# Raw words of the MLP weights in a room of their own, loaded one chunk ahead, converted among the first sequence's steps

## The chip, the core and the metric

The kernel runs on one core of a Trainium2 chip, with its five engines: TensorE (PE, matmuls; its weight loads are shown as PEld), VectorE (DVE), ScalarE (ACT), GpSimd (POOL) and SyncE (SP), whose queue issues all DMAs of this kernel. The metric is the device time of one execution in microseconds; what is compared is the median over runs.

## What is computed

The reference takes eight sequences of 3136 positions and 256 features. It is a spectral layer followed by a mixing layer with an MLP, cut here to what matters:

```python
X = np.fft.rfft(x, axis=1)                      # attention part
Yr = Xr @ w_r - Xi @ w_i + b_r
Yi = Xr @ w_i + Xi @ w_r + b_i
Yr, Yi = soft_threshold(Yr, 0.01), soft_threshold(Yi, 0.01)
x = np.fft.irfft(Yr + 1j * Yi, n=3136, axis=1)
mixed = np.real(np.fft.fft(np.fft.fft(x, axis=1), axis=2))
u = x + mixed
un = (u - mean(u)) / np.sqrt(var(u) + 1e-06)
out = u + np.maximum(un @ w_ch1, 0.0) @ w_ch2    # 256 -> 1024 -> 256
```

The MLP weights `w_ch1` and `w_ch2` come as 64-bit floats and reach the kernel as pairs of 32-bit words. Before the first MLP matmul the kernel has to make of them two single-precision parts, a high and a low one, with integer and float instructions.

## The kernel before

The sequence transform is split as 3136 = 64 x 49. Each sequence b goes through three parts, written as Python generators:

- `p1`: the transform over 64, from `in_x` (tile `xf`) by matmul (`g_f`) into `ev` and out to DRAM (`ad`). For b = 0 it is `p1_first`.
- `p2`, in four frequency steps q. `p2_f2` loads `af` (from `ad`) and the table `tff`, and does the transform over 49 (line 427); `p2_w` multiplies by the spectral weights (`g_w`, lines 150 to 152 by way of `mm3`), adds the bias (line 489, tile `y`) and thresholds; `p2_mix` forms sums `ef`, multiplies (`g_mix`, line 546) and combines the rows in `mq` on VectorE, GpSimd and ScalarE (lines 559 to 568), and stores them to DRAM (`md`, lines 573 to 587); `p2_yt` and `p2_g2` go back over 49 (table `tif`, result `bd`).
- `p3`, in groups of 3 or 4 rows: `p3_norm` loads `bf` (from `bd`) and `mt` (from `md`), does the last inverse transform (`g_g`, from the parts `bh` and `bl`), adds `mt` (line 691, tile `ut`) and normalizes (line 709, tile `nm`); `p3_tr` transposes (`g_ut`, line 727); `p3_mlp1` and `p3_mlp2` are the MLP (`h`, lines 150 to 152 and 746, 747; `o`).

Nearly every matmul from the second step on is done three times on split operands (`mm3`: high with low, low with high, high with high). The first sequence's own transforms over 64 and 49 and back are done once, on unsplit operands.

The order comes from two places. Each generator yields a due time in units where one sequence takes T = 10000, and a heap takes the piece of work with the earliest due time next. The first sequence's frequency steps have due times 1.0, 1.13, 1.26 and 1.39 T and run on for about 0.4 T each; its `p3` begins at 2.0 T, the second sequence's `p2` at 1.77 T. The framework's scheduler then sets the order on each engine. Every engine works through its own instructions in that order, and so does SP with its DMAs. A tile stands in a room that its tag names, with a number of buffers; an instruction that writes a buffer waits until the last reader of its earlier content is done. `behind(1, ...)` puts a DMA on SP's queue after the `af` load number 1.

`weights` loads and converts the MLP weights in eight chunks of 128 x 512 values (128 x 1024 words), four of `w_ch1` and four of `w_ch2`, due at 1.5 T and on in steps of 0.0525 T. `split_double` does one chunk. Its raw words stand in the tag `uth`, which the second and fourth frequency steps of the first sequence (`x_tiles`) and later the transposed MLP input use as well; its temporaries stand in `mt` and `ut`, which `p3_norm` uses as well. One chunk is one load, one Abs on ScalarE (line 169), seven instructions on VectorE (lines 170, 172, 174, 175, 178, 180, 182), one cast on ScalarE (line 186, the high part) and two instructions on GpSimd (lines 188 and 189, the low part).

## Time and profile before

| | |
|---|---|
| median of 3 runs | 1952.38 us (1949.41 to 1956.86) |
| the profiled execution's own time | 1949.14 us |
| its span | 1947.4 us |
| mean granted TensorE clock | 0.976 |
| PE busy | 1836.5 us (94%) |
| DVE busy | 1323.5 us (68%) |
| ACT busy | 850.1 us (44%) |
| POOL busy | 707.7 us (36%) |
| time of DMA packets, share of 16 engines' span | 42.3% (230.82 MB) |

A row of a group gives line, engine, operation, tiles (output and inputs), shapes and count, then busy us and mean ns of one, then the idle time of the engine before them and what ended it. Rows of the timeline give start and duration in us; "x4" merges four neighbours. A row of waits gives who waited for whom, the sum in us, the number of times and the longest. In the page's slices of 48.7 us each, TensorE is nearly full from the sixth on and has its holes in the first five.

### The profile page before, as it was taken

To read this page: it belongs to the slowest core of one execution; us is meant where nothing else is said; L and a number is where in the kernel's file an instruction comes from. 1 tells how busy PE (TensorE), PEld (TensorE's weight loads), DVE (VectorE), ACT (ScalarE), POOL (GpSimd) and SP (SyncE) were. 2 spreads that over 40 slices of the span, in tenths; PEclk is the share of its full clock that TensorE was granted. 3 is DMA by queue.
4 is the path that set the end of the run, shared out by engine and by line. 5 is a ranking of instruction groups with operands and counts; after the bars stand their busy time and mean duration, and the time that the engine had idled before them with its cause. 6 is when DMAs were issued, how large, how long until landed. Compare 5 with 4: busy or idle time off the path is not lost.

```text
span 1947.4 us, 34761 instructions
## 1 busy us (share of the span) xinstructions
PE 1836.5 (94%) x12115; PEld 1693.2 (87%) x12115; DVE 1323.5 (68%) x2831; ACT 850.1 (44%) x1888; POOL 707.7 (36%) x1087
## 2 busy tenths in 40 slices
PE   4972799999999999999999999999999999999999
PEld 2862799989999999998999999998999999998999
DVE  2677688767767677767677676666777776675543
ACT  2553454445444454444444444444544434433322
POOL 0336453344433344343333443324533332322210
PEclk7995899999999999999999999999999999999999
DMA  8685444255443544435443453435443333223210
GB/s 221 168 236 160 106 135 133 81 142 139 115 123 109 146 137 113 115 99 148 128 136 103 122 150 104 132 101 149 127 116 104 97 109 90 79 73 113 63 41 25
DMA packets 163538, 233.03 MB, mean 120 GB/s; under 512 B 27484, under 2 KB 107428, under 8 KB 163364
## 3 DMA queue, kind: packets, MB, share of 16 engines
q1 hardware_dynamic: 163364, 230.82, 42.3%
q8 instruction: 96, 1.57, 0.3%
q14 instruction: 78, 0.64, 0.1%
HBM read 127.95 MB, written 102.76 MB: 118 GB/s over the span
## 4 chain that ended last, share of the span: by engine, by line
PE 80%; DVE 6%; DMA 6%; SPq 3%; issue 2%; POOL 1%; ACT 1%; DVEq 0%; POOLq 0%; ACTq 0%
PE o L151 8%; PE o L150 8%; PE o L152 8%; PE h L150 8%; PE h L151 8%; PE h L152 8%; PE g_f L427 4%; PE g_w L150 3%; PE g_w L152 3%; PE g_w L151 3%; PE g_yt L617 2%; PE g_g L150 2%; PE g_g L152 2%; PE g_g L151 2%; PE g_ut L727 2%
## 5 line engine op out<-in xcount | busy, mean ns | idle before, releaser
L151 PE MATMUL o<-w2h,hl 128*128 128x256 f32 x1568 | 430.3, 284 | 9.7 <-DVE hl L747 9.7
L747 DVE SCALAR_TENSOR_TENSOR hl<-h,hh 128x512 fp32r<-128x512 f32 (+1 forms) x416 | 272.3, 655 | 236.9 <-ACT hh L746 235.7
L746 ACT ACTIVATE hh<-h 128x512 fp32r<-128x512 f32 (+1 forms) x416 | 237.7, 572 | 438.4 <-PE h L152 381.6
L152 PE MATMUL o<-w2h,hh 128*128 128x256 f32 x1568 | 422.5, 279 | 0.0
L150 PE MATMUL o<-w2l,hh 128*128 128x256 f32 x1568 | 396.7, 285 | 4.5 <-DVE ut L766 2.8
L150 PE MATMUL h<-utl,w1h 128*128 128x512 f32 (+1 forms) x832 | 322.8, 388 | 6.6 <-DVE hl L747 6.6
L152 PE MATMUL h<-uth,w1h 128*128 128x512 f32 (+1 forms) x832 | 316.7, 381 | 0.0
L151 PE MATMUL h<-uth,w1l 128*128 128x512 f32 (+1 forms) x832 | 316.4, 380 | 0.0
L151 PEld LDWEIGHTS o<-w2h,hl 128*128 128x128 f32 x1568 | 295.9, 189 | 16.5 <-DVE hl L747 11.8
L150 PEld LDWEIGHTS o<-w2l,hh 128*128 128x128 f32 x1568 | 284.9, 189 | 17.9 <-ACT Xsh L436 2.9
L152 PEld LDWEIGHTS o<-w2h,hh 128*128 128x128 f32 x1568 | 295.8, 189 | 3.2
L147 POOL TENSOR_TENSOR bl<-bf,bh 128x512 fp32r<-128x512 f32 x104 | 129.7, 1247 | 301.9 <-ACT bh L686 301.7
L152 PEld LDWEIGHTS h<-uth,w1h 128*128 128x128 f32 x832 | 156.5, 188 | 23.9
L150 PEld LDWEIGHTS h<-utl,w1h 128*128 128x128 f32 x832 | 156.7, 188 | 21.4 <-DVE hl L747 7.5
L147 POOL TENSOR_TENSOR xl<-xf,xh 128x512 fp32r<-128x512 f32 (+1 forms) x75 | 98.5, 1313 | 202.1 <-ACT xh L370 197.1
L427 PEld LDWEIGHTS g_f<-tff,af 98*128 98x128 f32 x1024 | 144.5, 199 | 30.7 <-issue 20.4
L427 PE MATMUL g_f<-tff,af 98*128 98x100 f32 x1024 | 151.2, 278 | 20.9 <-DMA tff<-c_tf 11.9
L151 PEld LDWEIGHTS h<-uth,w1l 128*128 128x128 f32 x832 | 156.8, 188 | 13.5
L147 POOL TENSOR_TENSOR Xl<-xx,Xh 128x400 fp32r<-128x400 f32 (+1 forms) x96 | 107.6, 1123 | 83.6 <-ACT Xh L436 65.6
L691 DVE TENSOR_TENSOR ut<-g_g,mt 128x512 f32<-128x512 f32 x104 | 68.3, 657 | 96.1 <-PE g_g L152 69.9
L147 POOL TENSOR_TENSOR Xsl<-xs,Xsh 128x200 fp32r<-128x200 f32 x120 | 76.9, 641 | 153.3 <-ACT Xsh L436 144.2
L709 DVE TENSOR_SCALAR nm<-ut,ag,rs 128x256 f32<-128x256 f32 x196 | 90.0, 498 | 52.3 <-POOL rs L706 51.9
(155 smaller groups left out, 3793.2 us busy)
## 6 DMA issues: line engine op xcount, KB each, us to landing
bd<-bev SPq DMA_DIRECT2D x128, 196.0 KB
af<-ad SPq DMA_DIRECT2D x62, 392.0 KB
bf<-bd SPq DMA_DIRECT2D x184, 128.0 KB
out_dram<-ut SPq DMA_DIRECT2D x92, 256.0 KB
xf<-in_x SPq DMA_DIRECT2D x176, 128.0 KB
ad<-ev SPq DMA_DIRECT2D x168, 128.0 KB
md<-mq SPq DMA_DIRECT2D x112, 192.0 KB
mt<-md SPq DMA_DIRECT2D x416, 32.0 KB
```

The lines of the kernel that those rows point to most:

```text
L147: gp.tensor_sub(out_, full, hi.bitcast(F32))
L150: te.matmul(o, lh, rl, start=start, stop=False)
L151: te.matmul(o, ll, rh, start=False, stop=False)
L152: return te.matmul(o, lh, rh, start=False, stop=stop)
L427: te.matmul(g[:, o:o + 100], afs[s][:, ui * D + k * 128:ui * D + k * 128 + 128], tfs[s][:, ui], start=True, stop=True)
L617: te.transpose(gt[:100, (v * 2 + o) * 128:(v * 2 + o + 1) * 128], y[:, o, place].rearrange("p c j -> p (c j)"), ident)
L691: va.tensor_add(ut[:, :n], g[:, :w].rearrange("p (n d) -> p n d", d=D), mt[:, :n])
L709: va.tensor_scalar(nm[:, j], ut[:, j], ag[:, j, 0:1], rs[:, j], op0=ALU.subtract, op1=ALU.mult)
L727: te.transpose(gv[:, k, j * 128:(j + 1) * 128], nm[:, j, k * 128:(k + 1) * 128], ident)
L746: sc.activation(hh[:, :w], h[:, :w], AF.Relu)
L747: va.scalar_tensor_tensor(hl[:, :w], h[:, :w], 0.0, hh[:, :w].bitcast(F32), op0=ALU.max, op1=ALU.subtract)
```

## The change

The raw words of a chunk now take two tiles of 128 x 512 words, one in the tag `hh` and one in the tag `bf`, with two buffers each. Both tags exist before; until the first MLP matmul and the first `p3_norm` they stand mostly empty. The instructions that read raw words (the Abs on ScalarE, lines 174 and 180 on VectorE) are therefore done in two halves of 256 values. The load of chunk j + 1 is issued ahead of the conversion of chunk j. The due times become 1.14 T and on in steps of 0.065 T, so that all eight fall into the first sequence's frequency steps. The tiles of the converted weights are allocated at that earlier place. All values computed are the same.

```diff
@@ -122,6 +122,9 @@
 SHAPE0, STEP0 = (1.0, 1.069, 0.988), 0.13
 SHAPE, STEP1, STEP = (0.395, 0.569, 0.36), 0.2, 0.25
 START1, LEAD = 1.77, 1.48
+
+W_AT, W_STEP = 1.14, 0.065
+W_PAD = 32
 MLAG, NRM, TR = 0.874, -1.239, -0.993
 
 
@@ -162,22 +165,23 @@
         def tmp(tag, bufs, dt=I32):
             return sb.tile([128, 512], dt, tag=tag, bufs=bufs, name=f"cv_{name}_{tag}")
 
-        raw = sb.tile([128, 1024], I32, tag="uth", bufs=2, name="raw_" + name)
-        behind(1, out=raw.rearrange("p (f e) -> p f e", f=src.shape[1]), in_=src)
-        lo, hi = raw[:, 0::2], raw[:, 1::2]
+        halves = [(t[:, 0::2], t[:, 1::2], np.s_[:, 256 * e:256 * e + 256]) for e, t in enumerate(src)]
         tf = tmp("mt", 2, F32)
-        sc.activation(tf, hi.bitcast(F32), AF.Abs)
+        for lo, hi, at in halves:
+            sc.activation(tf[at], hi.bitcast(F32), AF.Abs)
         va.tensor_scalar(tf, tf, HI_MIN, HI_MAX, op0=ALU.max, op1=ALU.min)
         t = tf.bitcast(I32)
         va.tensor_scalar(t, t, 3, 0x7FFFFFFF, op0=ALU.logical_shift_left, op1=ALU.bitwise_and)
         w = tmp("ut", UTB)
-        va.tensor_scalar(w, hi, -0x80000000, 0x40000000, op0=ALU.bitwise_and, op1=ALU.bitwise_or)
+        for lo, hi, at in halves:
+            va.tensor_scalar(w[at], hi, -0x80000000, 0x40000000, op0=ALU.bitwise_and, op1=ALU.bitwise_or)
         va.tensor_tensor(w, w, t, op=ALU.bitwise_xor)
         wf = w.bitcast(F32)
         e = tmp("ut", UTB)
         va.tensor_scalar(e, w, -0x800000, None, op0=ALU.bitwise_and)
         r = tmp("mt", 2)
-        va.tensor_scalar(r, lo, 8, None, op0=ALU.logical_shift_right)
+        for lo, hi, at in halves:
+            va.tensor_scalar(r[at], lo, 8, None, op0=ALU.logical_shift_right)
         rf = tmp("ut", UTB, F32)
         va.scalar_tensor_tensor(rf, r, 2.0 ** -44, e.bitcast(F32), op0=ALU.mult, op1=ALU.mult)
 
@@ -770,18 +774,33 @@
     def weights():
         w1v = w1.bitcast(I32).rearrange("(k p) f -> p k f", p=128)
         w2v = w2.bitcast(I32).rearrange("(f p) e -> p f e", p=128)
-        parts1 = [(np.s_[:, k, q * 512:q * 512 + 512], w1v[:, k:k + 1, q * 1024:q * 1024 + 1024])
-                  for k in range(2) for q in range(2)]
-        parts2 = [(np.s_[:, f:f + 2, :], w2v[:, f:f + 2]) for f in range(0, 8, 2)]
-        for i, (name, shape, loads) in enumerate((("w1", [128, 2, FF], parts1), ("w2", [128, 8, D], parts2))):
-            if i:
-                sb.tile([128, 32], F32, tag="pad", bufs=1, name="pad")
-            h = sb.tile(shape, F32R, tag=f"W{2 * i}", bufs=1, name=name + "h")
-            l = sb.tile(shape, F32R, tag=f"W{2 * i + 1}", bufs=1, name=name + "l")
-            mlp_w[name] = h, l
-            for j, (sl, src) in enumerate(loads):
-                yield T * (1.5 + 0.42 * (4 * i + j) / 8)
-                split_double(name, h, l, sl, src)
+
+        todo = [("w1", np.s_[:, k, q * 512:q * 512 + 512], [w1v[:, k, (2 * q + e) * 512:(2 * q + e + 1) * 512] for e in range(2)])
+                for k in range(2) for q in range(2)]
+        todo += [("w2", np.s_[:, f:f + 2, :], [w2v[:, f + e] for e in range(2)]) for f in range(0, 8, 2)]
+        raw = {}
+
+        def load(j):
+            name, sl, srcs = todo[j]
+            raw[j] = []
+            for e, tag in enumerate(("hh", "bf")):
+                t = sb.tile([128, 512], I32, tag=tag, bufs=2, name="raw_" + name)
+                behind(1, out=t, in_=srcs[e])
+                raw[j].append(t)
+        yield T * (W_AT - W_STEP)
+        load(0)
+        for j, (name, sl, _) in enumerate(todo):
+            yield T * (W_AT + W_STEP * j)
+            if j % 4 == 0:
+                i, shape = ((0, [128, 2, FF]), (1, [128, 8, D]))[j // 4]
+                if i and W_PAD:
+                    sb.tile([128, W_PAD], F32, tag="pad", bufs=1, name="pad")
+                h = sb.tile(shape, F32R, tag=f"W{2 * i}", bufs=1, name=name + "h")
+                l = sb.tile(shape, F32R, tag=f"W{2 * i + 1}", bufs=1, name=name + "l")
+                mlp_w[name] = h, l
+            if j + 1 < len(todo):
+                load(j + 1)
+            split_double(name, h, l, sl, raw.pop(j))
 
 
     tasks = [load_small(), load_consts(), weights()]
```

The framework's scheduler makes these orders of it. First SP's queue behind the stores of the first sequence's `p1` (`ad`); `raw_w` is a raw load, and in the change a number in a name tells the two tiles of a chunk apart. Before:

```order
L336 DMA ad_82<-ev 2x24x256
L413 DMA tff<-c_tf 98x400 x2
L262 DMA tif<-c_ti 100x392 x2
L413 DMA tff<-c_tf 98x400
L411 DMA af<-ad_81 98x1024 x2
L262 DMA xf<-in_x 64x512 x4
L411 DMA af<-ad_81 98x1024
```

Now:

```order
L340 DMA ad_80<-ev 2x24x256
L266 DMA raw_w_263<-in_w 128x512
L266 DMA raw_w_265<-in_w 128x512
L417 DMA tff<-c_tf 98x400 x2
L266 DMA raw_w_321<-in_w 128x512
L266 DMA raw_w_323<-in_w 128x512
L417 DMA tff<-c_tf 98x400
L415 DMA af<-ad_79 98x1024 x2
L266 DMA xf<-in_x 64x512 x4
L266 DMA raw_w_424<-in_w 128x512
L266 DMA raw_w_426<-in_w 128x512
L415 DMA af<-ad_79 98x1024
```

The first two chunks' loads stand ahead of the `af` loads of the second frequency step, the third's ahead of the next one, and the two `tif` loads have moved behind them.

Second, VectorE around the first bias add (`y`) of the first sequence. Before:

```order
L454 TENSOR_TENSOR xs<-g_f_275,im 128x200
L144 TENSOR_TENSOR Xl<-g_f_275,Xh 128x2x200
L489 SCALAR_TENSOR_TENSOR y_341<-g_w,bias,ks 128x400
L491 TENSOR_SCALAR m<-y_341 128x400
L492 TENSOR_TENSOR Y<-y_341,m 128x8x50
L449 TENSOR_TENSOR xs<-xx 128x200 x2
L489 SCALAR_TENSOR_TENSOR y_379<-g_w,bias,ks 128x400
```

Now, `cv_w` being the conversion's temporaries and 424 and 426 the third chunk's tiles:

```order
L184 TENSOR_SCALAR cv_w_mt<-raw_w_424 128x256
L177 TENSOR_SCALAR cv_w_ut<-raw_w_426 128x256
L184 TENSOR_SCALAR cv_w_mt<-raw_w_426 128x256
L172 TENSOR_SCALAR cv_w_mt<-cv_w_mt 128x512
L174 TENSOR_SCALAR cv_w_mt<-cv_w_mt 128x512
L493 SCALAR_TENSOR_TENSOR y_369<-g_w,bias,ks 128x400
L178 TENSOR_TENSOR cv_w_ut<-cv_w_ut,cv_w_mt 128x512
L495 TENSOR_SCALAR m<-y_369 128x400
```

Two whole chunks and six instructions of the third (24 in all) stand ahead of the first bias add; from there to just behind the ninth bias add, VectorE's instructions of the other chunks alternate with those of the frequency steps.

Third, VectorE at the first sequence's last combination of rows (`mq_1277` before, `mq_1415` now). Before:

```order
L559 TENSOR_TENSOR mq_1277<-g_mix_1464,mq_1277 100x1
L562 TENSOR_TENSOR mq_1277<-mq_1277 100x4x64 x2
L178 TENSOR_SCALAR cv_w1_ut_1197<-cv_w1_ut_1194 128x512
L449 TENSOR_TENSOR xs_1526<-xx_1527 128x200
L182 SCALAR_TENSOR_TENSOR cv_w1_ut_1201<-cv_w1_mt_1199,cv_w1_ut_1197 128x512
L174 TENSOR_SCALAR cv_w1_ut_1284<-raw_w1_1278 128x512
L180 TENSOR_SCALAR cv_w1_mt_1289<-raw_w1_1278 128x512
L170 TENSOR_SCALAR cv_w1_mt_1280<-cv_w1_mt_1280 128x512
L144 TENSOR_TENSOR til_1822<-tif_1819,tih_1821 100x392
L172 TENSOR_SCALAR cv_w1_mt_1280<-cv_w1_mt_1280 128x512
L567 COPY mq_1277<-mq_1277 100x4x127
```

Now:

```order
L563 TENSOR_TENSOR mq_1415<-g_mix_1542,mq_1415 100x1
L566 TENSOR_TENSOR mq_1415<-mq_1415 100x4x64 x2
L453 TENSOR_TENSOR xs_1604<-xx_1605 128x200
L571 COPY mq_1415<-mq_1415 100x4x127
L453 TENSOR_TENSOR xs_1632<-xx_1633 128x200
L695 TENSOR_TENSOR ut_1582<-g_g1_1578,mt_1565 128x512
```

The conversion's instructions are gone from between the combination and the first `ut` of `p3_norm`. TensorE's own instructions keep nearly the same order up to there and have the same one later.

## The prediction

> **What bounds the kernel now.** I read the page's slices first, then windows cut where the program's steps change, then the waits. The windows of core 0 (columns: stretch and length, busy us and instructions of each engine, granted TensorE clock, DMA share, GB/s):
>
> ```profile
> 36.00:51.50 15.50, 6.52 (x28) 6.27 (x28) 2.98 (x6) 4.21 (x12) 4.45 (x6) 0.53 0.80 207
> 51.50:88.70 37.20, 34.99 (x208) 29.98 (x208) 24.95 (x56) 22.19 (x63) 13.24 (x23) 1.00 0.63 174
> 88.70:120.00 31.30, 30.28 (x177) 25.79 (x177) 19.76 (x45) 18.11 (x49) 10.91 (x15) 1.00 0.69 195
> 120.00:142.60 22.60, 14.09 (x73) 10.53 (x72) 19.66 (x33) 12.43 (x29) 12.09 (x9) 0.92 0.89 263
> 142.60:153.10 10.50, 1.87 (x10) 1.62 (x8) 8.11 (x18) 4.98 (x13) 8.05 (x6) 0.50 0.85 257
> 153.10:214.10 61.00, 22.81 (x87) 20.39 (x87) 38.52 (x64) 17.12 (x32) 32.41 (x35) 0.58 0.43 117
> 214.10:1947.40 1733.30, 1707.16 (x11495) 1587.99 (x11493) 1201.41 (x2597) 762.63 (x1677) 626.33 (x992) 1.00 0.40 112
> ```
>
> TensorE bounds two stretches: from 51.5 to 120 us, where it is idle 3.2 of 68.5 us, and from 214.1 to the end, idle 26 of 1733. Between 120 and 214.1 it works 38.8 of 94.1 us, much of it at a granted clock near 0.5. Nothing this change touches can win more than those 55 idle us and the slow clock. The waits of TensorE between 120 and 215 us name what it stands for:
>
> ```profile
> PE g_ut L727 <- DVE nm L709: 24.5, 2, 13.0
> PE g_g L150 <- POOL bl L147: 22.3, 1, 22.3
> ```
>
> Both are the entry into the MLP of the first sequence: its inverse transform waits for `bl`, its transposes for the normalized rows. What makes these late is the conversion, whose eight chunks fill VectorE and GpSimd just there. VectorE's groups of that stretch (columns: busy us, mean ns):
>
> ```profile
> L174 DVE TENSOR_SCALAR cv_w_ut<-raw_w 128x512 int32<-128x512 int32 x8 | 8.4, 1048 | 0.7 <-DMA raw_w<-in_w 0.7
> L182 DVE SCALAR_TENSOR_TENSOR cv_w_ut<-cv_w_mt,cv_w_ut 128x512 f32<-128x512 int32 x8 | 7.5, 937 | 0.3
> L178 DVE TENSOR_SCALAR cv_w_ut<-cv_w_ut 128x512 int32<-128x512 int32 x8 | 6.9, 860 | 0.3
> L180 DVE TENSOR_SCALAR cv_w_mt<-raw_w 128x512 int32<-128x512 int32 x8 | 6.7, 836 | 0.0
> L170 DVE TENSOR_SCALAR cv_w_mt<-cv_w_mt 128x512 f32<-128x512 f32 x8 | 6.5, 811 | 0.8 <-ACT cv_w_mt L169 0.7
> L175 DVE TENSOR_TENSOR cv_w_ut<-cv_w_ut,cv_w_mt 128x512 int32<-128x512 int32 x8 | 5.8, 725 | 0.2
> L172 DVE TENSOR_SCALAR cv_w_mt<-cv_w_mt 128x512 int32<-128x512 int32 x8 | 4.3, 539 | 0.1
> ```
>
> The means add up to 5.76 us a chunk, 46 us in all. The last chunk ran with GpSimd quiet; its VectorE time in the windows of `cv_w_ut` and of `cv_w_mt` (VectorE first):
>
> ```profile
> 194.00:199.00 5.00, 2.24 (x4) 0.62 (x1) 0.79 (x1) 0.82 0.07 19
> 194.00:199.00 5.00, 2.65 (x5) 0.68 (x1) 0.82 0.07 19
> ```
>
> Lines 175 and 182 write one and read the other, so they stand in both, at 0.69 us each in that chunk: 2.24 + 2.65 - 1.38 = 3.5 us is the quiet price, against 5.76 on average.
>
> **The change part by part.** The order of TensorE's instructions is nearly row for row the same up to the MLP and identical later, so I move the times of a fixed chain and ask how much earlier the first MLP matmul (214.14) comes. All times are of the profiled execution, 1949.1 us with a span of 1947.4; the median of the runs shown, 1952.4, lies 3.2 above it.
>
> *Loads ahead of the second frequency step.* Four raw loads now stand before the `af` loads that TensorE waits for, and two `tif` loads move behind.
>
> ```profile
> raw_w<-in_w SPq DMA_DIRECT2D x8, 512.0 KB
> tif<-c_ti SPq DMA_DIRECT2D x11, 153.1 KB
> 38.00:47.00 9.00, 0.03 (x1) 0.02 (x1) 1.70 (x4) 1.74 (x7) 3.08 (x5) 0.50 0.84 216
> PE g_f L427 <- DMA af<-ad: 9.0, 1, 9.0
> ```
>
> Two chunks of 512 KB less two of 153 KB are 718 KB or 0.74 MB; at the 216 GB/s of that stretch 3.4 us, which passes straight to TensorE, since it waits for this load. With the two more instructions that the queue issues (some 0.4 us each) it is 4.2 at most, and nothing if the 16% of free DMA time takes it. I take 3.0.
>
> *Conversion among the first sequence's steps.* Two chunks and most of the third now stand ahead of the first bias add on VectorE, where it idled for about 11 us: nothing for these, as the raw words land while TensorE waits for `af`. The rest, three instructions and five whole chunks, is interleaved up to the ninth bias add, which ran here before:
>
> ```profile
> 88.72 0.63 DVE L489 SCALAR_TENSOR_TENSOR y<-g_w,bias,ks 128x400 f32<-128x400 f32 x1
> ```
>
> In 51.5 to 88.7 VectorE was idle 37.2 - 24.95 = 12.2 us. Quiet, the rest costs 1.8 + 5 x 3.5 = 19.3 us: TensorE falls 7.1 us behind. At the mean of before it is 2.5 + 5 x 5.76 = 31.3; the four half-width instructions that replace two add up to 0.6 a chunk (a half at a third more than half a whole): 34.3, or 22 us behind. I take 5.0 a chunk: GpSimd is about as busy (13.2 us plus 15 of conversion in some 52), but its own instructions here are short,
>
> ```profile
> L147 POOL TENSOR_TENSOR Xl<-xs,Xh 128x100 fp32r<-128x100 f32 x16 | 7.8, 509 | 10.5 <-ACT Xh L440 10.5
> ```
>
> so a VectorE instruction that runs into one waits less. 2.3 + 25 - 12.2 = 15 us behind. ScalarE (22 of 37 us busy) has room for its two half-width reads and a copy, some 1.3 us a chunk.
>
> The Trainium skill, "SBUF — State Buffer", section "SBUF: two separate sides", speaks against this part: VectorE instructions in a two-port mode, or with two SBUF inputs, and GpSimd instructions lock each other out of a shared port pair for a whole instruction. The trace agrees:
>
> ```profile
> 127.46 2.72 DVE L180 TENSOR_SCALAR cv_w_mt<-raw_w 128x512 int32<-128x512 int32 x1
> 128.62 1.27 POOL L147 TENSOR_TENSOR xl<-xf,xh 128x512 fp32r<-128x512 f32 x1
> ```
>
> An instruction that takes 0.42 us alone ends only after GpSimd's. With the lock at every turn the sum takes 22 us, without it 7.
>
> *What is freed at the end of the first sequence.* From 88.7 to the last mix matmul TensorE needs 31.3 us and then only the 14.1 busy us of the fourth window: 134.1 instead of 142.6. With 3 and 15 it is 152.1 (bounds 141.2 to 160.3). From that matmul to the first store of the mix it took 11.0 us, with GpSimd's difference held up behind the conversion; two steps earlier, without a conversion, the same took 6.1:
>
> ```profile
> 142.15 0.66 PE L546 MATMUL g_mix<-csf,ef 128*100 128x129 f32 x4
> 146.37 4.01 POOL L563 TENSOR_TENSOR mq<-mq 100x508 f32<-100x508 f32 x1 [1.42 <-ACT w1h L186]
> 153.16 0.31 SPq L573 DMA_DIRECT2D md<-mq  x1
> 105.64 0.60 PE L546 MATMUL g_mix<-csf,ef 128*100 128x129 f32 x4
> 111.71 0.49 SPq L573 DMA_DIRECT2D md<-mq  x1
> ```
>
> So the last window before the stores shrinks from 10.5 to 5.6: stores at 157.7 (146.8 to 165.9), which is later than before.
>
> *From the stores to the MLP* it took 61.0 us. What the chain needs:
>
> ```profile
> 155.80 0.76 SPq L587 DMA_DIRECT2D md<-mq  x1
> 136.57 2.99 DMA md<-mq
> 168.06 0.32 SPq L681 DMA_DIRECT2D mt<-md  x1
> 172.46 0.69 DVE L691 TENSOR_TENSOR ut<-g_g,mt 128x512 f32<-128x512 f32 x1 [0.32 <-DMA mt<-md]
> 184.58 0.66 PE L727 MATMUL g_ut<-ident,nm 128*128 128x128 f32 x2 [11.54 <-DVE nm L709]
> 201.63 0.69 DVE L691 TENSOR_TENSOR ut<-g_g,mt 128x512 f32<-128x512 f32 x1 [2.97 <-DMA mt<-md]
> 176.56 1.28 ACT L699 ACT_TABLE_LOAD   x1
> 205.62 0.66 PE L727 MATMUL g_ut<-ident,nm 128*128 128x128 f32 x2 [13.00 <-DVE nm L709]
> 214.14 0.47 PE L150 MATMUL h<-utl,w1h 128*128 128x512 f32 x1
> ```
>
> Stores issued, 3.4; landed, 3.0; `mt` issued to the first add, 4.4 (before, its issue waited until 168.06 for room that the conversion shares); add to transposes 4.0, as the second time, and 1.3 for the table load of the first; the second tile's 4.0 behind it; then 8.5 to the MLP. Together 28.6. Least 24.6, if the second tile overlaps; most 35.4, if the first tile again takes the 12.1 us from 172.46 to its transposes at 184.58. MLP at 157.7 + 28.6 = 186.3 (171.4 to 201.3): 27.8 us earlier (42.7 to 12.8). After that the order is the same and TensorE-bound, so it reaches the end: 1921.3 against the profiled execution, 1924 on the scale of the median.
>
> **The rivals.** *The conversion is nearly free* (0.17): quiet prices, no DMA delay, overlapped tail, 42.7 us, 1910. For it: 12 us idle on VectorE; against it: the contended mean. *The lock and the loads take most of it* (0.16): 4.2 and 22 us behind and a long first tile leave 12.8 us, 1940, or less if raw loads that wait for their room also hold the queue; for it speaks that the stores then come at 166, 13 us later than before. By the skill's rule named above it would go this way. *Slower* (0.07): the weight tiles are allocated earlier, so pools place them, and what follows, elsewhere; if the last window's matmuls ran 2.5% slower for their operands' places, 1707 x 0.025 = 43 us would outweigh the gain: 1967. It decides from 1.6% (27.8 of 1707). Nothing in the trace shows a rate that hangs on a place, hence the low chance. That the change doesn't do what it says is excluded by the order.
>
> **How the numbers follow.** The forecast has 0.60, with its own range 1912 to 1936. A measurement tells about 0.5%, 9.8 us, from no change, that is 1942.6. Faster: 0.60 + 0.17 + half of 0.16 = 0.85; same: the other half, 0.08; slower 0.07. The range 1907 to 1941 leaves out the slow rival, half of the one before it and the edge beyond full cover.
>
> **What would show it.** First MLP matmul near 186; TensorE's wait for `af` some 3 us longer than 9.0; between 50 and 105 us new waits of TensorE for VectorE, about 15 us, with VectorE over 90% busy; GpSimd's line 563 near 1.3 to 1.7 us in the last step; `mt` loads that no longer wait for VectorE; the stretch after the first MLP matmul still 1733 us. I am wrong if that last stretch changes by over 10 us, or if the stores come before 147 or after 166.

## The result and the profile after

The changed kernel takes 1939.72 us, the median of 6 runs (1934.24 to 1945.16), against 1952.39 us of the kernel before (6 runs beside it, 1948.85 to 1956.86): a ratio of 0.9935, with an interval of 0.9919 to 0.9951. It is 12.7 us faster. That lies inside the range (1907 to 1941) at its upper edge, though not in the forecast's own 1912 to 1936; the forecast was 1924, so the sign is right and the gain is less than half the size.

The profiled execution of it took 1938.88 us with a span of 1937.1, 10.3 us below that of before. The windows, cut at the first and the ninth bias add, the last mix matmul, the first store of the mix and the first MLP matmul (columns as in the windows of before):

```profile
36.00:57.31 21.31, 8.78 (x41) 7.70 (x40) 13.96 (x30) 8.85 (x24) 10.30 (x10) 0.58 0.95 248
57.31:112.36 55.05, 40.31 (x206) 30.96 (x206) 53.78 (x105) 29.00 (x84) 34.08 (x37) 0.97 0.64 171
112.36:156.94 44.58, 40.45 (x233) 33.55 (x234) 26.76 (x64) 24.85 (x64) 15.69 (x17) 1.00 0.72 206
156.94:166.38 9.44, 1.14 (x11) 0.97 (x9) 3.11 (x6) 4.32 (x11) 5.54 (x7) 0.82 0.63 190
166.38:199.06 32.68, 19.27 (x87) 16.67 (x88) 14.27 (x33) 11.51 (x23) 14.38 (x23) 0.74 0.59 149
199.06:1937.10 1738.04, 1711.28 (x11495) 1590.91 (x11493) 1200.49 (x2597) 763.81 (x1678) 627.32 (x993) 1.00 0.40 112
```

VectorE (third of the busy columns) is now full for 55 us, 53.78 of 55.05, where it idled for 12 of 37 us before, and that stretch takes 55 us where it took 37. The two windows between the last mix matmul and the MLP, 71.7 us before, take 42.1. The rest takes 1738.0 instead of 1733.3. What TensorE waits for, from 36 to 113 us and then from 126 to 200 us:

```profile
PE g_f L431 <- DMA af<-ad: 12.3, 1, 12.3
PE g_w L153 <- DVE y L493: 1.9, 2, 0.9
PE g_w L153 <- DVE ev L378: 1.7, 2, 1.5
PE g_g L153 <- POOL bl L150: 11.1, 1, 11.1
PE g_ut L731 <- DVE nm L713: 9.9, 2, 7.9
```

Both waits at the entry into the MLP have halved (22.3 and 24.5 us before); in exchange the wait for `af` is 3.3 us longer, and many short waits for VectorE have appeared in the frequency steps (8.7 us in all between 50 and 105 us; the two longest sums are shown). (Lines 150 to 152, 546, 691, 709 and 727 of before are 153 to 155, 550, 695, 713 and 731 now.)

Set against the prediction's chain, the profiled execution says where the missing gain is. It is four terms of similar size (17.5 us between these executions; some 15 between the medians, since the profiled execution of before lay 3.2 us below its median and this one 0.8):

| step | forecast | measured | late by |
|---|---|---|---|
| last mix matmul at | 152.1 | 156.94 | 4.8 |
| to the first store of the mix | 5.6 | 9.44 | 3.8 |
| stores to first MLP matmul | 28.6 | 32.68 | 4.1 |
| first MLP matmul to the end | 1733.3 | 1738.04 | 4.7 |
| sum before rounding (1921.3 forecast, 1938.9 measured) | | | 17.5 |

### The profile page after: what moved, and what is told of

It reads as the page before. It is cut to its first block, busy times and chain, and to the rows that moved or that the text cites. A ratio compares the mean times of both kernels' runs of the same rounds, so it can differ in the third digit from the quotient of the medians.

```text
span 1937.1 us, 34781 instructions
## 1 busy us (share of the span) xinstructions
PE 1841.4 (95%) x12115; PEld 1692.0 (87%) x12115; DVE 1320.5 (68%) x2847; ACT 850.6 (44%) x1896; POOL 707.5 (37%) x1087
## 4 chain that ended last, share of the span: by engine, by line
PE 75%; DVE 5%; DMA 4%; SPq 3%; issue 1%; POOL 1%; ACT 1%; DVEq 0%; POOLq 0%; ACTq 0%
PE o L154 8%; PE o L153 8%; PE o L155 8%; PE h L153 8%; PE h L154 8%; PE h L155 8%; PE g_f L431 4%; PE g_w L153 3%; PE g_w L155 3%; PE g_w L154 3%; PE g_g L153 2%; PE g_g L154 2%; PE g_g L155 2%; PE g_ut L731 2%; PE g_yt L621 2%; DMA md<-mq 1%
## 5 line engine op out<-in xcount | busy, mean ns | idle before, releaser
L153 PEld LDWEIGHTS h<-utl,w1h 128*128 128x128 f32 x832 | 157.1, 189 | 21.9 <-DVE hl L751 7.9
L431 PE MATMUL g_f<-tff,af 98*128 98x100 f32 x1024 | 149.8, 276 | 25.5 <-DMA af<-ad 12.3
```

The source lines that it names most:

```text
L153: te.matmul(o, lh, rl, start=start, stop=False)
L431: te.matmul(g[:, o:o + 100], afs[s][:, ui * D + k * 128:ui * D + k * 128 + 128], tfs[s][:, ui], start=True, stop=True)
```

## The experiments

All medians below stand against runs of the kernel before on the same chip; each ratio has its interval behind it. Milestones ("last mix", "stores", "MLP") are those of the table, from one profiled execution each.

### The parts alone

What does the new room do, and what do the new due times? The first run keeps the due times of before in the new room, the second is the kernel before with the new due times.

```diff
-W_AT, W_STEP = 1.14, 0.065
+W_AT, W_STEP = 1.5, 0.0525
```

> The changed kernel with the due times of before (1.5 T and on in steps of 0.0525 T): of the two parts of the change the room alone. Theory (the room is what lets the conversion go forward, the due times hardly matter, since the scheduler pulls ready work ahead): the conversion again stands between the first and the ninth bias add, 11 rows of it ahead of the first one instead of 24, so the first bias add comes at 54 to 56 us (57.3 in the changed kernel), the ninth within 4 us of 112.4, the first MLP matmul within 6 us of 199.1, the time within 0.4% of 1940. Rival (the due times do it): the conversion falls back into the end of the first sequence, the first MLP matmul comes at 210 or later, the time is near 1952.

```diff
 # in the kernel before
-                yield T * (1.5 + 0.42 * (4 * i + j) / 8)
+                yield T * (1.14 + 0.065 * (4 * i + j))
```

> The kernel before with the new due times: of the two parts of the change the due times alone; the raw words stay in the room that the second and fourth frequency steps use. Theory (the room sets the place): one chunk goes ahead of the first bias add, the other seven only from the eighth on, into the third and fourth frequency step, where VectorE had some 22 idle us between 88.7 and 142.6; the first bias add comes at 53 to 55 us, the ninth near 92, the last mix matmul at 150 to 160, the first MLP matmul at 195 to 205, the time at 1938 to 1945. Rival (what counts is that the conversion is done early, whatever the place): as the conversion still ends in the last mix step, the first MLP matmul stays near 214 and the time near 1952.

The room alone: 1953.06 us (ratio 1.0010, 0.9998 to 1.0022). The times alone: 1952.64 us (1.0007, 0.9995 to 1.0019). Neither gains anything, and both together gain 12.7. Yet each alone brings the first MLP matmul from 214.1 to about 203 us; each loses it again behind that matmul. The last window of the first and of the second run:

```profile
203.64:1950.80 1747.16, 1716.58 (x11502) 1595.31 (x11500) 1204.03 (x2598) 764.59 (x1678) 627.46 (x993) 1.00 0.40 111
202.89:1950.50 1747.61, 1721.86 (x11495) 1600.76 (x11493) 1204.40 (x2597) 764.19 (x1678) 625.52 (x993) 0.99 0.40 111
```

Both take some 14 us more than the 1733.3 of before. The trace of each kernel divides this last window (worked out over all its matmuls: waits of TensorE from the first `hl` on; half clock at half the length of its stretches, an estimate of the time that it costs; spacing as the difference from before in the distance of two matmul starts at full clock, times their number; the three account for each window's difference from before to within 1.2 us):

| us | last window | waits | lost to half clock | spacing |
|---|---|---|---|---|
| before | 1733.3 | 22.1 | 1.7 | 0 |
| the changed kernel | 1738.0 | 22.7 | 3.4 | +2.4 |
| the same program again | 1741.1 | 21.9 | 8.5 | +2.4 |
| room alone | 1747.2 | 26.4 | 6.8 | +3.3 |
| times alone | 1747.6 | 21.7 | 8.5 | +9.1 |
| tail closer (below) | 1742.9 | 24.0 | 6.8 | +2.8 |
| tail closer, four `bev` (below) | 1747.7 | 26.0 | 8.5 | +2.5 |
| more rooms (below) | 1742.6 | 18.5 | 3.4 | +11.6 |

The last row's execution took 1947.99 us, 5 us less than that kernel's median. With the room alone the scheduler dealt TensorE's first 500 or so instructions behind the first MLP matmul in another order, with some more of them left behind that point, and TensorE waits 4.3 us longer. With the times alone the order is that of the changed kernel but for a few neighbours; there the distance of the matmuls costs 9.1 us, of which the section on the hardware tells. What is lost to half clock differs by 5 us between two executions of one program, so that column says little about a kernel. So a conversion that is done early is not yet a gain: what counts is also which order the scheduler makes of it, and at which spacing the matmuls then run.

### What the conversion and the loads cost where they now stand

Here is the floor first: neither raw loads nor conversion; ScalarE fills the weight tiles from a table that is there anyway. What follows on it: the loads without the conversion (each raw tile is read by one instruction on one column); the conversion with only the first chunk loaded, so that all eight convert the same words; and the loads with ScalarE's copies in place of the conversion. These four leave out part of the computation as said; the last of them keeps ScalarE's reads of the raw words.

```diff
 # the floor
-        load(0)
-            if j + 1 < len(todo):
-                load(j + 1)
-            split_double(name, h, l, sl, raw.pop(j))
+            split_double(name, h, l, sl, ())      # two copies from K['wr'][0] on ScalarE
```

> The changed kernel with no raw loads and no conversion: ScalarE copies a constant into both weight tiles, two instructions of 0.62 us a chunk where it has three of 1.5 us in sum now. The weights are not the reference's. It is the floor for every way of placing the conversion. Theory (all of the delay up to the ninth bias add is conversion and loads): the first bias add at 51 to 52.5 us, the ninth at 88 to 91, the last mix matmul at 132 to 137, the first MLP matmul at 174 to 179 (the 41 to 43 us behind the last mix matmul stay), the time 20 to 26 us below the changed kernel. Rival (the run without conversion had its ninth bias add at 102 us for another reason, such as the new order): the ninth stays near 100 and the first MLP matmul near 188.

```diff
 # the loads alone: the floor, with every load, and of each raw tile
+            sc.activation(tf[:, i:i + 1], t[:, 1:2].bitcast(F32), AF.Abs)
```

> As the run with no loads and no conversion, but with all sixteen raw loads in their new places, each read by one single-column instruction so that its room comes free: the loads by themselves, with ScalarE as lightly loaded as there. If the loads cost by themselves (bytes and queue), the first bias add comes at 54 to 56 us and the ninth 45 us or more after it (99 or later), as in the run without conversion. If ScalarE's copies were what slowed that run between the two (it was full at 60 to 70 us there), the first bias add is still at 54 to 56, but the ninth comes 37 to 40 us after it (91 to 96).

```diff
 # the conversion alone
-            if j + 1 < len(todo):
-                load(j + 1)
-            split_double(name, h, l, sl, raw.pop(j))
+            split_double(name, h, l, sl, raw[0])
```

> The changed kernel with the raw words of the first chunk alone loaded (once), and all eight chunks converted from them: 7 of the 8 pairs of loads are left out, so the weights are not the reference's; the conversion's instructions all stay. In the run without conversion the ninth bias add still came at 102.0 us, 13.3 later than before, so the loads look to be the larger half of the delay. Theory (the loads, by their share of the DMA time and by holding SP's queue while they wait for room): the first bias add comes at 52 to 55 us, the ninth at 96 to 102 instead of 112.4, the first MLP matmul 8 to 15 us earlier than 199.1, the time 6 to 13 us below the changed kernel. Rival (VectorE alone sets the pace, the loads are hidden beside it): the first bias add earlier by 3, the ninth at 107 to 111, the time within 5 us of the changed kernel.

```diff
 # all loads, ScalarE's copies in place of VectorE's and GpSimd's instructions
+            sc.activation(wf[at], hi.bitcast(F32), AF.Abs)
...
+        sc.copy(l[sl], v(wf))
```

> The changed kernel with all of VectorE's and GpSimd's conversion left out: the raw words are loaded as before, and ScalarE copies their upper halves into both weight tiles, so the weights are not the reference's. It gives the whole price of the conversion in its new place, and what the loads and the way from the last mix matmul to the MLP cost without it. Theory: the first bias add at 54 to 56 us (the loads ahead of af stay), the ninth at 91 to 95, the last mix matmul at 134 to 142; from there to the first MLP matmul 40 to 43 us as in the changed kernel (42.5), since nothing of the conversion stands there; first MLP matmul at 176 to 184, time 15 to 22 us below the changed kernel. Rival (the way to the MLP is slow because of what the conversion left behind: buffers, loads, GpSimd): that way shrinks to the forecast 34 us or less, the first MLP matmul at 168 to 175.

| | last mix | MLP | median us | ratio |
|---|---|---|---|---|
| floor | 138.5 | 180.1 | 1922.01 | 0.9847 (0.9830 to 0.9865) |
| loads alone | 143.8 | 186.4 | 1926.22 | 0.9863 (0.9842 to 0.9884) |
| loads and ScalarE's copies | 146.8 | 189.7 | 1926.75 | 0.9882 (0.9855 to 0.9909) |
| conversion, one load | 158.7 | 199.7 | 1941.65 | 0.9952 (0.9932 to 0.9973) |
| the changed kernel | 156.9 | 199.1 | 1939.72 | 0.9935 (0.9919 to 0.9951) |

Between floor and changed kernel lie 18.4 us at the last mix matmul, 19.0 at the MLP and 17.7 in the medians: that is the price of the conversion and its loads at their new place (the floor still has sixteen copies on ScalarE, so it may lie a little high and the price a little low). The loads alone cost 5.3 of it at the last mix, but they do not add to the conversion: with one load instead of eight the last mix comes no earlier (158.7). They are hidden behind it. From the run with ScalarE's copies, the first of the four to be made, I had concluded that the loads were the larger part of what it left; that fell with the other three (ScalarE's copies themselves had filled ScalarE in places: 10.0 us of the 10 from 60 to 70).

The floor, in the same cuts, holds the answer to the other question, where the forecast gain went:

```profile
53.55:92.00 38.45, 34.92 (x208) 29.90 (x207) 24.81 (x56) 22.33 (x63) 13.18 (x23) 1.00 0.62 174
92.00:138.49 46.49, 41.87 (x248) 34.98 (x247) 26.84 (x62) 27.29 (x71) 16.05 (x19) 1.00 0.72 207
138.49:147.35 8.86, 1.14 (x11) 0.97 (x9) 3.13 (x6) 4.32 (x11) 5.55 (x7) 0.69 0.61 179
147.35:180.06 32.71, 21.14 (x87) 18.39 (x88) 14.60 (x33) 11.44 (x23) 14.60 (x23) 0.67 0.59 148
```

With no conversion anywhere, the way from the last mix to the MLP still takes 8.9 + 32.7 = 41.6 us; the changed kernel takes 42.1. The prediction had 34.2.

To see how far one execution of the same program stands from another, the changed kernel was run again:

> The changed kernel once more, for how far two executions of one program differ in the marks used here. If the marks are the program's: the first bias add, the ninth, the last mix matmul and the first MLP matmul within 1.5 us of 57.3, 112.4, 156.9 and 199.1, and 1738 us behind the first MLP matmul within 1.5. If the 4.8 us by which that last stretch was longer than before the change are of the execution, it now lies anywhere from 1733 to 1742.

1939.96 us (0.9928, 0.9904 to 0.9951), the MLP at 200.3 and 1741.1 us behind it, 3.1 more than the first time, with 5.1 us more lost to half clock. So a last window that differs by 3 us says nothing by itself.

### The way from the last mix to the MLP

What holds the 42 us? The timeline of the changed kernel, from the last mix matmul to the first store:

```profile
156.60 0.61 PE L550 MATMUL g_mix<-csf,ef 128*100 128x129 f32 x4
159.15 0.59 ACT L652 COPY bev<-g_g 98x512 f32<-98x512 f32 x1 [2.71 <-DMA bd<-bev]
160.05 0.59 ACT L652 COPY bev<-g_g 98x512 f32<-98x512 f32 x1
160.79 0.39 ACT L557 COPY mq<-g_mix 100x256 f32<-100x256 f32 x1
162.57 1.26 POOL L567 TENSOR_TENSOR mq<-mq 100x508 f32<-100x508 f32 x1 [0.75 <-ACT mq L569]
166.38 0.38 SPq L577 DMA_DIRECT2D md<-mq  x1
```

ScalarE has to copy the mix product out of PSUM (line 557). It comes to this only at 160.79, since two copies for `bd` stand ahead of it in its queue, and the first of these waits until an earlier `bd` store has left one of the two `bev` buffers. From the copy to the store it is 5.6 us. In the kernel before, ScalarE made this copy ahead of both `bev` copies, 1.6 us behind the last mix matmul:

```profile
144.11 0.36 ACT L553 COPY mq<-g_mix 100x256 f32<-100x256 f32 x1
144.38 0.59 ACT L648 COPY bev<-g_g 98x512 f32<-98x512 f32 x1
```

So the wait for the `bd` store came with the new order; the conversion had not covered it. The test gives `bev` two more buffers, in a tag that is empty then:

```diff
-                bev = sb.tile([98, 512], F32, tag="bev", bufs=2, name="bev")
+                bev = sb.tile([128, 512], F32, tag="hl" if b == 0 and q >= 2 and i % 2 else "bev", bufs=2, name="bev")[:98]
```

> The changed kernel with four buffers instead of two for the first sequence's bev in the last two frequency steps (every second one stands in the tag hl, which is free there). In the changed kernel ScalarE's copy of the last mix product stands behind two bev copies, and the first of them waits 2.7 us for an earlier store to land. Theory (that wait is what makes the last mix matmul to the first store 9.4 us instead of the 5.6 forecast): it becomes 5.6 to 6.6 us, the stores come 3 to 4 us earlier (162 to 163.5), the first MLP matmul too (195 to 196.5), the time 2 to 4 us below the changed kernel. Rival (the chain of GpSimd and VectorE instructions behind it is as long): it stays above 8 us and nothing comes earlier.

In its timeline:

```profile
158.04 0.59 ACT L652 COPY bev<-g_g 98x512 f32<-98x512 f32 x1 [1.31 <-DMA bd<-bev]
158.78 0.38 ACT L557 COPY mq<-g_mix 100x256 f32<-100x256 f32 x1
```

The last mix comes at 156.69 (the last of its four in the group's row; 156.94 in the changed kernel), so the copy runs 2.1 us behind it instead of 3.9; the stores come 7.6 us behind the last mix instead of 9.4, and the MLP at 196.1. The median is 1938.16 (0.9926, 0.9906 to 0.9947): 1.6 us less than without, which these intervals alone do not tell apart. The first `bev` copy still waits 1.31 us here, so this edit takes away only part of the delay.

Behind the stores, the first tile's add (`ut`), its transposes (`g_ut`) and the second tile's matmul and add:

```profile
177.43 0.68 DVE L695 TENSOR_TENSOR ut<-g_g,mt 128x512 f32<-128x512 f32 x1
174.78 1.27 POOL L150 TENSOR_TENSOR bl<-bf,bh 128x512 fp32r<-128x512 f32 x1 [4.37 <-DMA mt<-md]
182.35 0.66 PE L731 MATMUL g_ut<-ident,nm 128*128 128x128 f32 x2 [7.88 <-DVE nm L713]
184.09 0.63 PE L153 MATMUL g_g<-bl,invh 128*128 128x512 f32 x1
185.60 0.69 DVE L695 TENSOR_TENSOR ut<-g_g,mt 128x512 f32<-128x512 f32 x1 [0.59 <-PE g_g L155]
```

The second tile's `bl` is ready at 176.05, and TensorE stands idle for 7.88 us before 182.35; but the second tile's matmul `g_g` stands behind the first tile's transposes in the written order, and so runs at 184.09. The test lets the first group's steps follow each other closer:

```diff
-                yield t0 + T3 * (NRM + i / 4)
+                yield t0 + T3 * (NRM + i / (16 if b == 0 and gi == 0 else 4))
```

> The changed kernel with the second tile of the first group of the first sequence normalized earlier (its due time a sixteenth of a group later per half tile instead of a quarter), so that its inverse transform stands ahead of the first tile's transposes on TensorE. Theory (the way from the stores to the MLP is 32.7 us instead of 28.6 because the second tile's inverse transform waits behind the first tile's transposes): the second tile's add comes at 180 to 183 us instead of 185.6, the first MLP matmul at 194 to 197 instead of 199.1. What the rest of the program makes of it is open, as the order of the later instructions is dealt anew: kept order would give a time 2 to 5 us below the changed kernel; the two halves of the change run alone had a remainder 9 to 10 us longer than the changed kernel's, and with as much lost here the time would be 5 to 8 us above it.

```profile
178.77 0.69 DVE L695 TENSOR_TENSOR ut<-g_g,mt 128x512 f32<-128x512 f32 x1 [4.07 <-DMA mt<-md]
181.47 0.69 DVE L695 TENSOR_TENSOR ut<-g_g,mt 128x512 f32<-128x512 f32 x1 [0.16 <-issue]
183.47 0.66 PE L731 MATMUL g_ut<-ident,nm 128*128 128x128 f32 x2 [6.51 <-DVE nm L713]
```

The second add now comes 2.7 us behind the first instead of 8.2, and stores to MLP take 28.2 us. That is close to the prediction's 28.6, but by other terms: the second tile's transposes come 7.1 us behind the first's and the MLP 5.2 behind those, where it had 4.0 and 8.5. Both edits together:

> The four bev buffers and the earlier second tile together, all values computed. From the last mix matmul to the stores 7.6 us and from there to the MLP 28.2, as in the two runs alone: 36, the first MLP matmul at 191 to 194 us. If what stands behind the first MLP matmul lasts as long as in the changed kernel (1738 us): the time 5 to 7 us below it. If the order dealt anew costs again what it cost the earlier second tile alone (1743 us): within 2 us of it.

Stores to MLP 27.6 us, last mix to MLP 36.4, MLP at 192.7, 6.3 us earlier than in the changed kernel. But the medians are 1940.92 (0.9937, 0.9911 to 0.9964) and 1941.46 (0.9936, 0.9914 to 0.9957), nothing gained: behind the first MLP matmul the two take 1742.9 and 1747.7 us instead of 1738.0. As with the room alone, the scheduler dealt TensorE's next few hundred instructions in another order, with some more left behind the cut, and the waits there grow by 1.3 and 3.3 us (table above); the rest of it is half clock, which may be of these executions. The wait is found and removed, and its gain doesn't reach the end; for how much of that the new order stands, these runs don't settle.

The opposite test puts the last two chunks behind the third step's mix stores, with the four `bev` buffers:

```diff
-                behind(1, out=t, in_=srcs[e])
+                behind(1 if j < 6 else ("m", 0, 2), out=t, in_=srcs[e])
...
+            yield from after(("af", 1 if j + 1 < 6 else ("m", 0, 2)))
```

> The changed kernel with the four buffers for bev, and with the last two chunks loaded behind the mix stores of the third frequency step and converted between the last combinations of rows; six chunks stay where the change put them. All values computed. With no conversion at all the first MLP matmul came at 180.1 us, with eight chunks early and four bev buffers at 196.1: 2 us a chunk. If each chunk taken out of the early steps gives that back, and two fit into VectorE's pauses behind the last mix matmul: the ninth bias add at 105 to 108 us, the first MLP matmul at 191 to 194, the time 2 to 4 us below that of the run with four bev buffers alone (1938.2). If the chunks hold up the last combination as they did before the change: from the last mix matmul to the first store over 9.5 us, the first MLP matmul at 196 or later, no gain.

1944.49 us (0.9952, 0.9933 to 0.9970). The last mix is 4.2 us earlier (152.7), but from there to the stores it takes 15.6 us, as the late chunks hold the last combination, and TensorE waits longer for `bl` than with all chunks early (11.1):

```profile
PE g_g L153 <- POOL bl L150: 17.8, 1, 17.8
```

### Spreading the conversion otherwise

Three runs place the same work differently: paced by the `af` loads of the steps; paced and with four `bev` buffers; and more rooms: the chunks of `w2` come first and are loaded into the room that the converted `w1` takes later, those of `w1` into the two tags as now.

```diff
 # paced (with four bev buffers: (1, 1, 5, 5, 7, 7, 7, 7))
-                behind(1, out=t, in_=srcs[e])
+                behind((1, 1, 5, 5, 5, 7, 7, 7)[j], out=t, in_=srcs[e])
...
+                yield from after(("af", (1, 1, 5, 5, 5, 7, 7, 7)[j + 1]))
```

> The changed kernel with the raw loads tied to later af loads: chunks one and two as now, chunks three to five behind the fifth af load counted from zero, six to eight behind the seventh; 18 conversion rows then stand ahead of the first bias add instead of 24, none until the fourth, and the last ones at the thirteenth instead of the ninth. With one load for all chunks the ninth bias add came no earlier (110.2 us), so the loads are not what sets the pace there. Theory (VectorE has no pause between the first and the ninth bias add and every us put there goes to TensorE, while it idles from the ninth on): the first bias add at 54 to 56 us (57.3 in the changed kernel), the ninth at 98 to 105 instead of 112.4, the last mix matmul at 149 to 154 instead of 156.9, the first MLP matmul at 191 to 196 instead of 199.1, the time 3 to 8 us below the changed kernel. Rival (the same work costs as much later, since the steps behind are as tight): the last mix matmul stays at 156 to 158 and the time within 2 us of the changed kernel.

> Both at once, all values computed: the raw loads paced still later (chunks three and four behind the fifth af load, five to eight behind the seventh) and the four buffers for bev. If the two gains are of different places they add: the last mix matmul at 148 to 153 us, from it to the first store 6 to 8, the first MLP matmul at 187 to 193, the time 6 to 11 us below the changed kernel. If the conversion that now reaches the last mix step holds up what follows it, as it did before the change, the way from the last mix matmul to the stores grows past 9 us and the time comes within 3 us of the changed kernel.

```diff
 # more rooms
+        todo = todo[4:] + todo[:4]
...
+                if j < 4:
+                    if e == 0 and j % 2 == 0:
+                        wide.append(sb.tile([128, 4, 512], I32, tag=("W1", "W0")[j // 2], bufs=1, name="raw_" + name))
+                    t = wide[-1][:, 2 * (j % 2) + e]
```

> The changed kernel with more rooms for raw words: the four chunks of the second matrix come first and are loaded into the room where the first matrix's weights go later, the chunks of the first matrix into the two tags as now; six of eight pairs of loads then wait for no reader. All bytes are loaded, all values computed. If the loads cost because they wait for their room and hold SP's queue: the ninth bias add at 102 to 107 us instead of 112.4, the first MLP matmul at 190 to 195 instead of 199.1, the time 4 to 9 us below the changed kernel. If they cost by the bytes that share the DMA engines with af: the ninth bias add within 3 us of 112.4, the time within 4 us of the changed kernel.

Paced: 1942.88 us (0.9949, 0.9930 to 0.9968); with more `bev` buffers 1939.68 (0.9937, 0.9913 to 0.9961). The ninth bias add comes 12 us earlier in both (100.4 instead of 112.4), the last mix only 1.7 and 5.6 us earlier: most of what a later conversion saves in the second step it takes again in the third and fourth. The later conversion with four `bev` buffers also lost what these had given: it took 9.7 us from the last mix to the stores. More rooms: 1952.85 us (1.0002, 0.9987 to 1.0018), the whole gain lost: the MLP comes 4.4 us later (203.5), and behind it the spacing alone costs 11.6 us, 9.2 more than in the changed kernel.

### GpSimd's part

While VectorE is full, its own instructions beside the conversion's are longer. VectorE's groups of the changed kernel from 42 to 112 us (busy us, mean ns), and then the same sums `ef` in the kernel before from 42 to 92 us:

```profile
L177 DVE TENSOR_SCALAR cv_w_ut<-raw_w 128x256 int32<-128x256 int32 x16 | 8.0, 522 | 5.1 <-DMA raw_w<-in_w 5.1
L184 DVE TENSOR_SCALAR cv_w_mt<-raw_w 128x256 int32<-128x256 int32 x16 | 7.5, 496 | 0.0
L186 DVE SCALAR_TENSOR_TENSOR cv_w_ut<-cv_w_mt,cv_w_ut 128x512 f32<-128x512 int32 x7 | 6.1, 875 | 0.1
L178 DVE TENSOR_TENSOR cv_w_ut<-cv_w_ut,cv_w_mt 128x512 int32<-128x512 int32 x8 | 5.8, 730 | 0.1
L531 DVE SCALAR_TENSOR_TENSOR ef<-Y,mask 128x200 f32<-128x200 f32 x8 | 5.6, 740 | 0.0
L181 DVE TENSOR_SCALAR cv_w_ut<-cv_w_ut 128x512 int32<-128x512 int32 x8 | 4.8, 604 | 0.1
L172 DVE TENSOR_SCALAR cv_w_mt<-cv_w_mt 128x512 f32<-128x512 f32 x8 | 4.4, 548 | 0.0
L174 DVE TENSOR_SCALAR cv_w_mt<-cv_w_mt 128x512 int32<-128x512 int32 x8 | 3.3, 416 | 0.1
```

```profile
L527 DVE SCALAR_TENSOR_TENSOR ef<-Y,mask 128x200 f32<-128x200 f32 x8 | 3.3, 438 | 0.3 <-POOL Y L496 0.2
```

A chunk costs VectorE twice 0.522 and 0.496 and once the other five, 5.2 us, and `ef` goes from 438 to 740 ns. Is it GpSimd that stretches them? The first run leaves out GpSimd's part of the conversion (the low part then lacks the rest of the high part, and is a copy on ScalarE); the second gives it to the full VectorE; the third does so with four `bev` buffers, and the fourth is the third again.

```diff
 # without GpSimd
-        d = tmp("ut", UTB, F32)
-        gp.tensor_sub(v(d), v(wf), h[sl].bitcast(F32))
-        gp.tensor_add(l[sl], v(d), v(rf))
+        sc.copy(l[sl], v(rf))
 # the low part on VectorE
-        gp.tensor_sub(v(d), v(wf), h[sl].bitcast(F32))
-        gp.tensor_add(l[sl], v(d), v(rf))
+        va.tensor_sub(v(d), v(wf), h[sl].bitcast(F32))
+        va.tensor_add(l[sl], v(d), v(rf))
```

> The changed kernel without GpSimd's two instructions per chunk: the low part of a weight is then only the tail bits that VectorE forms, copied by ScalarE; the remainder of rounding the high part is left out. Theory (VectorE's instructions are stretched by GpSimd's conversion running beside them): VectorE's price of a chunk falls from 5.1 us to 3.6 to 4.2, the ef instructions from 740 ns to about 450, the ninth bias add comes at 98 to 104 us instead of 112.4, the first MLP matmul at 184 to 192, the time 8 to 14 us below the changed kernel. Rival (the stretch comes from the step's own traffic, or the delay from loads): the price of a chunk stays above 4.8 us, the ninth bias add within 3 us of 112.4, the time within 4 us of the changed kernel.

> The changed kernel with the low part of the weights on VectorE alone, bev left with two buffers: one edit out of the two of the run that came 8 us below the changed kernel. If GpSimd's two instructions cost the more by stretching VectorE's: the ninth bias add at 102 to 106 us, the first MLP matmul at 196 to 198 (193.5 with the bev buffers, which alone gave 3.0), the time 4 to 8 us below the changed kernel (1940). If the two edits help only together: the first MLP matmul at 198 or later, the time within 2 us of the changed kernel.

> The four bev buffers, and the low part of the weights (two instructions a chunk) on VectorE instead of GpSimd; all values computed. Leaving these two out gave 6.4 us at the ninth bias add and 5.0 at the first MLP matmul. On VectorE they are two instructions of 0.69 us (the duration of a 128x512 addition with two inputs there): 1.4 us a chunk, 11 in all, against the stretch that they cause from GpSimd. If that stretch is the larger: the conversion's sum on VectorE at 42 to 44 us with GpSimd's two gone, the ninth bias add at 108 to 111, the first MLP matmul at 193 to 196, the time 0 to 3 us below the run with four bev buffers alone. If VectorE's own work is: the ninth bias add at 113 or later, the first MLP matmul at 197 or later.

> Both edits once more (low part on VectorE, four buffers for bev), in more rounds and beside the one without the buffers: 1930 to 1934 us if the 1931.8 of its first run are the program's; the difference to the run beside it, 1 to 4 us, is what the bev buffers are worth there.

Without GpSimd's part: 1935.24 us (0.9923, 0.9899 to 0.9947), 4.5 less than the changed kernel, with the conversion at 32.0 us on VectorE, or 4.0 a chunk. With it on VectorE: 1938.05 (0.9929, 0.9910 to 0.9948). With it on VectorE and four `bev` buffers: 1931.77 (0.9885, 0.9865 to 0.9905), and again 1934.09 (0.9908, 0.9888 to 0.9929). VectorE's groups of the third run, 42 to 121 us:

```profile
L177 DVE TENSOR_SCALAR cv_w_ut<-raw_w 128x256 int32<-128x256 int32 x16 | 4.6, 311 | 3.0 <-DMA raw_w<-in_w 3.0
L531 DVE SCALAR_TENSOR_TENSOR ef<-Y,mask 128x200 f32<-128x200 f32 x8 | 4.1, 556 | 0.0
L184 DVE TENSOR_SCALAR cv_w_mt<-raw_w 128x256 int32<-128x256 int32 x16 | 4.0, 281 | 0.0
L192 DVE TENSOR_TENSOR cv_w_ut<-cv_w_ut,w1h 128x512 f32<-128x512 f32 x4 | 3.4, 838 | 2.4 <-ACT w1h L190 2.4
```

The engine that was full took on two more instructions a chunk (some 0.7 to 0.8 us each), and the ninth bias add came 9.8 us earlier than in the changed kernel (102.6 instead of 112.4): the half-width reads fall from 522 and 496 to 311 and 281 ns, `ef` from 740 to 556. So GpSimd's instructions did stretch VectorE's. The traces show it instruction by instruction: of the changed kernel's 32 half-width reads, the 16 that overlap an instruction of GpSimd take 734 ns on average (280 to 1390), the other 16 284; in the third run only two overlap one. It is not GpSimd's part of the conversion alone, though. In the run without that part `ef` was still 705 ns, where some 450 had been expected, since two of the eight meet GpSimd's own combination of rows and end 0.2 us behind it (the other six average 464):

```profile
103.72 1.38 POOL L568 TENSOR_TENSOR mq<-mq 100x508 f32<-100x508 f32 x1
102.54 2.78 DVE L531 SCALAR_TENSOR_TENSOR ef<-Y,mask 128x200 f32<-128x200 f32 x2
```

The Trainium skill, "Perfetto Trace Analysis", section "Optimizing Scalar/DVE Operations", warns that moving work between these two might not help, as they share a port; here moving it off GpSimd, onto the busier engine, cost nothing and, with four `bev` buffers, helped.

The ten runs of this version have a median of 1932.1 us, the ten of the changed kernel 1940.0. It is the fastest of all that compute everything: 7.9 us below the changed kernel and about 20 below the kernel before. Alone, its two edits gave 1.6 and 1.7 us, less together than 7.9; medians of so few runs differ by 2 to 3 us, so whether they add more than their sum is open.

## Why the prediction was right in sign and short in size

**Loads ahead of `af`.** Forecast 3.0 us; TensorE's wait for `af` grew from 9.0 to 12.3 (9.7 in the floor, 12.1 with the loads alone). Right. But "nothing for these" on the first two and a half chunks was not: the third chunk's words were late,

```profile
55.00 0.29 DVE L177 TENSOR_SCALAR cv_w_ut<-raw_w 128x256 int32<-128x256 int32 x1 [2.41 <-DMA raw_w<-in_w]
```

and the first bias add, queued behind that chunk on VectorE, came at 57.3, 5.7 us later than before and not 3: a term of some 2 us that was set at nothing. The runs that leave work out divide the 5.7 in another way. The floor's first bias add stands at 53.55 and that of the loads alone at 55.54, so 2.0 us are there without either, 2.0 are the loads' and 1.8 the conversion's; where the first 2.0 come from is open.

**The conversion among the steps.** Forecast 5.0 us a chunk and TensorE 15 us behind from the first to the ninth bias add; measured 5.2 a chunk with VectorE full, and 17.9 behind (55.05 instead of 37.13), inside the bounds of 7 and 22. The price of a chunk was right. What had no term was VectorE's own work, which stretches beside GpSimd (`ef` 438 to 740 ns), and one window at half clock (80.8 to 84.3 us). The prediction weighed such a stretch by way of the lock, for the conversion's instructions alone.

**The last mix.** Forecast 152.1, measured 156.9: 2.7 and 2.9 us from the two steps above, and 0.8 less than the 45.4 that were left for the stretch behind them. The sum against the run without loads and conversion is 18.4, as good as the forecast's 3 + 15; but that run's last mix stands at 138.5 and not at the 134.1 that the prediction began from, so by it 4.4 of the 4.8 us are there without the change. Its copies on ScalarE may be part of that, and which of the two readings holds is open. The two terms were in any case not independent: alone the loads cost 5.3 and the conversion 20.2 (158.7 less 138.5).

**The step that failed** is what was said to be freed: "the last window before the stores shrinks from 10.5 to 5.6", and "together 28.6" from the stores to the MLP. They took 9.4 and 32.7, and 8.9 and 32.7 with no conversion at all: 7.9 of the 12.8 us by which the first MLP matmul came late. For the first I had taken over the 6.1 us of a step two steps earlier, where ScalarE copied the mix product 0.4 us behind the last mix matmul. In the new order that copy stands behind two `bev` copies, the first of which waits 2.7 us for a `bd` store, and it comes 3.9 us behind; the order of before had it ahead of both. Four buffers win back 1.8 us of the 3.8. For the second I had added the shortest latencies of a chain. From the stores to the first add it took 11.1 us (forecast 10.8), from there to its transposes 4.9 (5.3), to the second tile's transposes 9.5 (4.0) and to the MLP 7.2 (8.5). So the term that failed is the 4.0 by which the second tile was to follow the first. In the written order its matmul stands behind the first tile's transposes, and its add comes 8.2 us behind; this order allows 33 us, and the tests that reorder it took 28.

**After the MLP.** Forecast 1733.3, and a change of over 10 us was to be the sign of being wrong; measured 1738.0, and 1741.1 in the second execution. Of the 4.7 us the spacing of the matmuls is 2.4, half clock 1.7 and waits 0.6. The order was that of before, but for neighbours that change places in the first 500 or so instructions; the time was not quite.

**The rivals.** The result stands nearest to "the lock and the loads take most of it", 1940, and the time was that of this rival, though not by its road alone: loads and conversion took 18 to 23 us (by the floor's run, and by the two steps above less 0.8), where the rival has 4.2 + 22, the way from the last mix to the MLP took 7.9 us more than the forecast, and what stands behind it 4.7. That the time lies in the range at all is owed to its upper edge, which was there for this rival. The stores came at 166.4, just past the 166 that I had named as the bound. The slower rival, tile places, was given 0.07 since nothing in the trace showed a rate that hangs on a place. A rate that differs from kernel to kernel exists (below), though that the place is its cause is not shown. In the changed kernel it is worth some 2 us, in two of the experiments 9 to 12. Of the signs named in advance these came: the wait for `af`, VectorE over 90% busy, GpSimd's instruction in the last combination at 1.26 us, and `mt` loads right behind the stores (172.96 for the first, 3.5 us behind the last store). TensorE's new waits for VectorE came too, but as 8.7 us and not 15; the MLP near 186 and the 1733 us behind it did not.

## What to carry to other kernels

What a removed cost frees must be read from the changed kernel's written order of the queues behind it, with every instruction that stands ahead of the one that matters, and not from the shortest latency of the chain or from another step of the kernel before; a run that leaves the work out altogether shows that floor directly, and here it shows the 41.6 us of the last stretch that the forecast took for 34.2. A scheduler that deals the order anew can give back 10 us of a local gain somewhere else, so compare the order and the spacing of the matmuls behind the change before believing its local price. And where VectorE is full, look at what GpSimd does beside it before moving work to GpSimd.
